# RWKV7 with a gated feed-forward on one core: weights converted by VectorE and ScalarE, in four parts, with the second stage starting two chunks earlier

## The chip, the cores and the metric

The kernel runs on one core of a Trainium2 chip. The metric is the device time of one execution in microseconds (us). Before the change three runs took 1106.02, 1109.82 and 1111.58 us, median 1109.82. A core has five engines with an instruction stream each: TensorE (PE, with its weight loads, PEld, shown apart), VectorE (DVE), ScalarE (ACT), GpSimd (POOL) and SyncE (SP), which here only issues DMAs. They meet through semaphores.

## The reference

Two stages. The first is a recurrence over 768 tokens for 4 batches and 8 heads of width 40; its output, as 3072 tokens of 320 numbers, is the input of a feed-forward with g = h·cos(h):

```python
for t in range(S):
    y[:, :, t] = np.einsum('bhd,bhde->bhe', rt, state)
    Sa = np.einsum('bhde,bhe->bhd', state, at)
    state_decay = state * wt[:, :, None, :] - np.einsum('bhd,bhe->bhde', Sa, bt)
    state = state_decay + np.einsum('bhd,bhe->bhde', vt, kt)
...
x = np.ascontiguousarray(attn_out.transpose(0, 2, 1, 3)).reshape(B * S, H * D)
...
h = x @ w_in
g = h * np.cos(h)
return (g @ w_out).astype(np.float32)
```

r, k, v, w, a, b are float32. w_in (320 x 2048) and w_out (2048 x 320) come as float64: the seeded array of float32 was multiplied by a float64 scalar. They are turned into float32 on the chip.

## The kernel before

**The recurrence** is cut into 24 chunks of 32 tokens (C = 32, NCH = 24). Chunk c works in segments. p1 prepares two chunks at a time: `p1_w` turns the decay w and scans it, `p1_a` makes the reciprocal `rw` and `aT`, `p1_b` turns `bn` into `bT`, `p1_n` makes the matrix `nps` from which `u` is filled through DRAM (`nd`). For four chunks at once a triangular system is inverted on VectorE in 31 steps of two instructions (`inv_step`, lines 309 and 313; tiles `inv_tmp` and `inv`), and sent through DRAM (`rd`) into `rt` (lines 317 and 320). p2 prepares one chunk: `p2_v` loads k, v and r of the next chunk and has GpSimd copy v and r into the padded tiles `vp` and `rp` (line 331), which TensorE turns to `vT` and `rT`; `p2_k` and `p2_g` follow. The chain that carries the state from chunk to chunk is `ch_t` (TensorE turns the state, `sT`, line 385: the mark by which a chunk's beginning is read), `ch_q` (`qps`), `ch_x` (`x0ps`, and x copied by ScalarE and VectorE), `ch_s` (`sps` with `rt`, then `sm`), `ch_z` (`dps`, the new state `qz` and the output `yt`). The output goes through DRAM (`xd`, line 492) into `xT` (lines 499 and 501), which holds two chunks.

**The second stage** (called MoE in the names) works on 12 groups of two chunks, g, and four blocks of 512 hidden columns, j. For each of the 48 pairs `first_a` and `first_b` make `ph` = w_in times xT (24 matmuls: 16 with `w_in_sb`, 8 with `w_in_tail`), ScalarE and VectorE turn it into g·cos (tiles `turns` and `gT`), and `second`, twice, adds `gT` times `w_out_sb` to `po` (16 matmuls). These four calls are pieces, 192 in all. They are laid between the segments of the chunks by a rule: from chunk START on, after each segment, as many as are due by SHARE pieces per chunk, and none of a group before the chunk that follows its second one. The rest comes behind chunk 23.

**The order.** TensorE keeps the order of the program text, segment by segment. The other engines' instructions are ordered by a scheduler, each engine then runs its own in that order.

**The weights.** `load_weights` (before the loop over chunks) goes through four blocks j; each has seven conversions by `rounded`: two of `w_in_sb` (128 x 512), one of `w_in_tail` (128 x 256), four of `w_out_sb` (128 x 320). A conversion loads the 64-bit words by a DMA of ScalarE's queue (line 163) into a tile `words` that shares the two buffers of `gT`; mantissa (`mant`, in the three buffers of `turns`) and exponent (`expo`, in the two buffers of `nt`) are taken apart by VectorE (lines 168, 169, 173, 178), scaled by ScalarE (line 172), the exponent is limited and moved by GpSimd (lines 176, 177), and GpSimd multiplies both (line 181). `kept` makes tiles that live throughout, and fills them by VectorE.

Of the kernel before, what the change touches and what calls it, by code (L numbers as in the profile page):

```python
# [20 lines left out]
def kernel(  # L21
# [63 lines left out]

    def kept(name, shape, n=1, fill=None, part=lambda t: t):

        tiles = []
        for i in range(n):
            t = const.tile(shape, F32, tag=f"{name}{i}", name=f"{name}{i}")  # L90
            if fill is not None:
                nc.vector.memset(part(t), fill)
            tiles.append(t)
        return tiles
# [21 lines left out]
    def load(c, names, via=nc.sync):  # L116
        for n in names:
            for i in range(B):
                via.dma_start(
                    nat[n][c % 2][blk[i], :, :D],  # L120
                    src[n][i, :, c * C : (c + 1) * C, :].rearrange("h t d -> t h d"),
                )
# [19 lines left out]
    rnd = kept("rnd", [P, 1], 1, ROUND)[0]  # L142
    w0 = kept("w0", [P, 4 * B, C], 1, 0.0)[0]
    w1 = kept("w1", [P, 4 * B, C], 1, 0.0)[0]
    bn_b = kept("bn", [P, H, DP], 7, 0.0, padding)
# [8 lines left out]
    by_in = kept("by_in", [P, 1], 1, 0.5 / math.pi)[0]  # L154
    by_out = kept("by_out", [P, 1], 1, 2.0 * math.pi)[0]

    def rounded(dst, src, by, by_sb):


        n, wid = dst.shape[0], dst.shape[-1]  # L160
        words = sb2.tile([P, 512, 2], I32, tag="gT", name="words")[:n, :wid]
        for rows, part in src:
            nc.scalar.dma_start(words[rows].rearrange("p n w -> p (n w)"), part.bitcast(I32))
# [4 lines left out]
        nc.vector.tensor_scalar(mant, hi, 0xFFFFF, None, ALU.bitwise_and)  # L168
        nc.vector.scalar_tensor_tensor(
            frac, lo.bitcast(U32), 2.0**-32, mant, ALU.mult, ALU.add  # L170
        )
        nc.scalar.activation(frac, frac, ACTF.Identity, bias=by_sb[:n], scale=2.0**-20 * by)
        nc.vector.tensor_scalar(
            expo, hi, 20, 0x7FF, ALU.logical_shift_right, ALU.bitwise_and
        )
        nc.gpsimd.tensor_scalar(expo, expo, 1023.0 + 128, 1023.0 - 127, ALU.min, ALU.max)
        nc.gpsimd.tensor_scalar(expo, expo, 127.0 - 1023, 2.0**23, ALU.add, ALU.mult)
        nc.vector.scalar_tensor_tensor(
            expo, hi, -(2**31), expo, ALU.bitwise_and, ALU.bitwise_or
        )  # L180
        nc.gpsimd.tensor_tensor(dst, frac, expo.bitcast(F32), ALU.mult)

    def load_weights():

# [9 lines left out]

        for j in range(NF // 4):
            cs = slice(4 * j * P, 4 * (j + 1) * P)
            for i in range(2):
                put(w_in_sb[:, i, cs], [(every, moe_w_in[i * P : (i + 1) * P, cs])], 0.5 / math.pi, by_in)
            put(
                w_in_tail[:, j].rearrange("p f n -> p (f n)"),  # L200
                [
                    (full[e], moe_w_in[2 * P :, (4 * j + 2 * e) * P : (4 * j + 2 * e + 2) * P])
                    for e in range(2)
                ],
                0.5 / math.pi, by_in,
            )
            for f in range(4 * j, 4 * j + 4):
                put(w_out_sb[:, f, :], [(every, moe_w_out[f * P : (f + 1) * P, :])], 2.0 * math.pi, by_out)

# [117 lines left out]
    def p2_v(c):  # L327
        load(c + 1, "kvr") if c + 1 < NCH else None
        nc.gpsimd.tensor_tensor(unpad(kn_b[c % 2]), unpad(nat["k"][c % 2]), G["rw", c], ALU.mult)  # L329
        for dst, m in ((vp, "v"), (rp, "r")):  # L330
            nc.gpsimd.tensor_copy(  # L331
                dst.rearrange("p (i f) d -> p f i d", f=2)[:, :, :, :D],
                nat[m][c % 2].rearrange("p (f i) d -> p f i d", f=2),
            )
        nc.gpsimd.tensor_copy(vvm[c % 2][:, :, C : C + D], nat["v"][c % 2])
        ps = at("vT")
# [245 lines left out]
    with tc.manual_schedule(engines={mybir.EngineType.PE}):  # L582
# [78 lines left out]
```

## Time and profile before

| what | before |
|---|---|
| runs | 1106.02, 1109.82, 1111.58 us; median 1109.82 |
| the profiled execution | 1102.25 us |
| its span on the core | 1100.5 us |
| mean granted TensorE clock | 0.812 |
| busy TensorE, VectorE, ScalarE, GpSimd | 74%, 46%, 31%, 21% |
| chunk 1 opens (first sT) | 178.33 us |
| chunk 2, chunk 3, chunk 4 open | 213.67, 231.93, 260.05 us |
| chunk 23 opens | 1020.8 us |

A row of the timeline reads: start in us, length in us, engine, line, operation, output<-inputs, shape, count, and in brackets the idle time of the engine before it with what ended it. A row of a group reads: line, engine, operation, shape and count, then total busy us and the mean ns of one, then the idle time just before them with its causes. A row of the stretches reads: from:to, length, then busy time (and number of instructions) of PE, PEld, DVE, ACT and POOL, the granted TensorE clock as a share of full speed, the DMA engines' busy share and GB/s.

### The profile page before, as it was taken

Reading aid. Unit: us, or ns where it says so; the run is one execution under the profiler, and the core shown is the slowest. Engines: PE = TensorE matmul, PEld = TensorE weight load, DVE = VectorE, ACT = ScalarE, POOL = GpSimd, SP = SyncE. Lnnn points to the kernel's source line nnn. Section 1 sums busy time; section 2 is a strip of 40 time slices with the busy share of each in tenths; the row PEclk is TensorE's granted clock in tenths of the full one; section 3 lists DMA queues with packets and bytes.
Section 4 is the critical chain, followed back from the end, with each engine's and each line's share of the span. In section 5 each row is a group of like instructions: output and inputs, shape, how many; then the busy total and the mean of one; then the engine's idle time right before and its main releaser. Section 6 shows DMA issues by size and latency. Waiting matters only on the chain.

```text
span 1100.5 us, 36921 instructions
## 1 busy us (share of the span) xinstructions
PE 819.2 (74%) x16472; PEld 630.7 (57%) x16472; DVE 511.2 (46%) x1107; ACT 342.4 (31%) x651; POOL 233.9 (21%) x414
## 2 busy tenths in 40 slices
PE   4310036666897898887888797797897789998997
PEld 3210035555676666665666666675665567776775
DVE  6489662464525563424572424662424662333221
ACT  2021121123233424232433242333232333434443
POOL 2454651312203012112011202111202111111000
PEclk8555556556888988797988988997889989998999
DMA  4554533235123323232232223141221221000000
GB/s 98 84 126 107 141 79 61 45 65 98 23 45 62 52 65 70 41 64 60 42 65 53 35 48 76 30 88 34 40 52 34 38 68 36 28 16 8 22 26 13
DMA packets 235519, 61.66 MB, mean 56 GB/s; under 512 B 209504, under 2 KB 229472, under 8 KB 235360
## 3 DMA queue, kind: packets, MB, share of 16 engines
q1 hardware_dynamic: 229088, 48.48, 23.4%
q10 hardware_dynamic: 6272, 10.82, 3.3%
q8 instruction: 130, 2.13, 0.8%
q14 instruction: 29, 0.24, 0.1%
HBM read 45.09 MB, written 14.16 MB: 54 GB/s over the span
## 4 chain that ended last, share of the span: by engine, by line
PE 59%; DVE 19%; ACT 8%; DMA 5%; issue 5%; POOL 3%; SPq 1%; ACTq 0%; DVEq 0%; POOLq 0%
PE ph L97 20%; PE po L97 19%; DVE inv L313 4%; DVE inv_tmp L309 3%; PE gram L97 3%; DVE rw L251 3%; PE x0ps L97 3%; PE vT L216 2%; ACT turns L529 2%; ACT turns L530 2%; PE sT L385 2%; PE dps L97 2%; PE nps L97 2%; PE bT L216 2%; PE qps L97 2%
## 5 line engine op out<-in xcount | busy, mean ns | idle before, releaser
L97 PE MATMUL po<-w_out_sb,gT 128*128 128x320 f32 x768 | 250.0, 479 | 2.3 <-issue 2.3
L97 PE MATMUL ph<-xT,w_in_sb 128*128 128x256 f32 x768 | 198.5, 410 | 0.5 <-issue 0.5
L97 PEld LDWEIGHTS po<-w_out_sb,gT 128*128 128x128 f32 x768 | 155.5, 211 | 71.6 <-issue 27.2
L528 DVE SCALAR_TENSOR_TENSOR turns<-turns,ph 128x512 f32<-128x512 f32 x96 | 61.6, 683 | 233.4 <-ACT turns L527 233.4
L97 PEld LDWEIGHTS ph<-xT,w_in_sb 128*128 128x128 f32 x768 | 154.7, 207 | 26.6 <-issue 0.9
L527 ACT ACTIVATE turns<-ph,rnd 128x512 f32<-128x512 f32 x96 | 60.7, 684 | 160.6 <-PE ph L97 160.6
L531 DVE TENSOR_TENSOR gT<-ph,turns 128x512 f32<-128x512 f32 x96 | 65.8, 689 | 63.0 <-ACT turns L530 62.7
L313 DVE TENSOR_TENSOR inv<-inv,inv_tmp 128x31 f32<-128x31 f32 (+15 forms) x186 | 73.8, 397 | 5.0
L309 DVE TENSOR_TENSOR inv_tmp<-u,inv 128x31 f32<-128x31 f32 (+15 forms) x186 | 70.7, 380 | 5.1
L530 ACT ACTIVATE turns<-turns,half_pi 128x512 f32<-128x512 f32 x96 | 68.9, 722 | 2.1
L97 PE MATMUL gram<-aT,kT 40*32 40x32 f32 x1536 | 20.1, 224 | 58.4 <-DVE yt L481 41.5
L529 ACT ACTIVATE turns<-turns 128x512 f32<-128x512 f32 x96 | 59.5, 623 | 13.1 <-DVE turns L528 13.1
L475 POOL TENSOR_TENSOR qz<-qz,wc 128x160 f32<-128x160 f32 x92 | 40.0, 460 | 105.2 <-DVE qz L474 105.1
L239 POOL COPY wx<-wp 128x496 f32<-128x496 f32 x24 | 14.8, 615 | 212.7 <-DVE wp L235 211.4
L251 DVE RECIPROCAL rw<-wn 128x320 f32<-128x320 f32 x24 | 51.6, 2150 | 12.1 <-PE wn L216 12.0
L97 PE MATMUL ph<-xT,w_in_tail 64*128 64x256 f32 x384 | 56.3, 413 | 0.0
L97 PEld LDWEIGHTS gram<-aT,kT 40*32 40x32 f32 x1536 | 17.3, 125 | 63.1 <-issue 42.3
L216 PE MATMUL vT<-ident,vp 128*128 128x128 f32 x96 | 18.0, 319 | 46.3 <-POOL vp L331 46.3
L329 POOL TENSOR_TENSOR kn<-nat_k,rw 128x320 f32<-128x320 f32 x24 | 21.0, 873 | 142.1 <-PE dps L97 142.0
L331 POOL COPY vp<-nat_v 128x320 f32<-128x320 f32 x24 | 10.9, 455 | 184.9 <-PE vT L216 72.2
L216 PE MATMUL vT<-ident,rp 128*128 128x128 f32 x96 | 17.2, 310 | 43.9 <-POOL rp L331 43.9
L264 ACT COPY bT<-bT 128x512 f32<-128x512 f32 x24 | 14.0, 585 | 110.8 <-PE bT L216 110.8
(94 smaller groups left out, 1170.9 us busy)
## 6 DMA issues: line engine op xcount, KB each, us to landing
words<-in_moe_w_out_dram ACTq DMA_DIRECT2D x16, 320.0 KB
words<-in_moe_w_in_dram ACTq DMA_DIRECT2D x8, 512.0 KB
nat_w<-in_w_dram SPq DMA_DIRECT2D x96, 40.0 KB
nat_b<-in_b_dram SPq DMA_DIRECT2D x96, 40.0 KB
nat_k<-in_k_dram SPq DMA_DIRECT2D x96, 40.0 KB
nat_v<-in_v_dram SPq DMA_DIRECT2D x96, 40.0 KB
nat_r<-in_r_dram SPq DMA_DIRECT2D x96, 40.0 KB
xd<-yt SPq DMA_DIRECT2D x48, 80.0 KB
```

The costliest lines, as they stand in the source:

```text
L97: nc.tensor.matmul(o, lhsT=lhsT, rhs=rhs, start=start, stop=stop, skip_group_check=True)
L216: nc.tensor.transpose(ps[:, i * P : (i + 1) * P], x[:, 2 * i : 2 * i + 2].rearrange("p e d -> p (e d)"), ident)
L251: nc.vector.reciprocal(rw, unpad(ps[:, 0].rearrange("p (h d) -> p h d", h=H)))
L309: nc.vector.tensor_tensor(tmp, u[:, :j, j : j + 1].to_broadcast([P, j, C - j]), x[:, j : j + 1, j:].to_broadcast([P, j, C - j]), ALU.mult,)
L313: nc.vector.tensor_tensor(x[:, :j, j:], x[:, :j, j:], tmp, ALU.subtract)
L385: nc.tensor.transpose(ps[:, i // 4, (i % 4) * P : (i % 4 + 1) * P], qz[:, i // 2, i % 2, C : C + P], ident)
L475: nc.gpsimd.tensor_tensor(z, z, wc.rearrange("p (f m b) -> p f m b", f=2, m=2)[:, :, :, bb] .unsqueeze(3).to_broadcast([P, 2, 2, D]), ALU. ...
L527: nc.scalar.activation(n, u, ACTF.Identity, bias=rnd, scale=1.0)
L528: nc.vector.scalar_tensor_tensor(n, n, -ROUND, u, ALU.add, ALU.subtract)
L529: nc.scalar.activation(n, n, ACTF.Abs)
L530: nc.scalar.activation(n, n, ACTF.Sin, bias=half_pi, scale=-2.0 * math.pi)
L531: nc.vector.tensor_tensor(G["gT", j][:, 2 * e : 2 * e + 2].rearrange("p f t -> p (f t)"), u, n, ALU.mult)
```

## The change

Five edits. **Conversion:** GpSimd's three steps go. The exponent is taken first; limiting and moving it is one Relu of ScalarE with the bias tile `to_bits`, and the last multiply is VectorE's. `expo` has buffers of its own. **Parts:** `load_weights` takes a block j; block 0 is converted before the loop, block c at the beginning of chunk c for c = 1, 2, 3. **START** is 2 instead of 4, so SHARE is 7.71 pieces per chunk instead of 8.48. **Fills** are GpSimd's but for three tiles. **k, v, r** have one buffer instead of two, and the next chunk's loads stand behind the copies in `p2_v`.

```diff
-    def kept(name, shape, n=1, fill=None, part=lambda t: t):
+    def kept(name, shape, n=1, fill=None, part=lambda t: t, on=nc.gpsimd):
...
-                nc.vector.memset(part(t), fill)
+                on.memset(part(t), fill)
...
-    nat = {n: kept(f"nat_{n}", [P, H, DP], 2, 1.0 if n == "w" else 0.0, padding) for n in "wabk"}
-    nat |= {n: kept(f"nat_{n}", [P, H, D], 2) for n in "vr"}
+    nat = {n: kept(f"nat_{n}", [P, H, DP], 2, 1.0, padding, nc.vector) for n in "w"}
+    nat |= {n: kept(f"nat_{n}", [P, H, DP], 2, 0.0, padding) for n in "ab"}
+    nat |= {n: kept(f"nat_{n}", [P, H, D], 1) for n in "kvr"}
...
+    to_bits = kept("to_bits", [P, 1], 1, (127.0 - 1023) * 2**23)[0]
...
-        expo = sb2.tile([P, 512], I32, tag="nt", name="expo")[:n, :wid]
+        expo = sb2.tile([P, 512], I32, tag="expo", name="expo")[:n, :wid]
         frac = mant.bitcast(F32)
+        nc.vector.tensor_scalar(
+            expo, hi, 20, 0x7FF, ALU.logical_shift_right, ALU.bitwise_and
+        )
+        nc.scalar.activation(expo, expo, ACTF.Relu, bias=to_bits[:n], scale=2.0**23)
         nc.vector.tensor_scalar(mant, hi, 0xFFFFF, None, ALU.bitwise_and)
         nc.vector.scalar_tensor_tensor(
             frac, lo.bitcast(U32), 2.0**-32, mant, ALU.mult, ALU.add
         )
         nc.scalar.activation(frac, frac, ACTF.Identity, bias=by_sb[:n], scale=2.0**-20 * by)
-        nc.vector.tensor_scalar(
-            expo, hi, 20, 0x7FF, ALU.logical_shift_right, ALU.bitwise_and
-        )
-        nc.gpsimd.tensor_scalar(expo, expo, 1023.0 + 128, 1023.0 - 127, ALU.min, ALU.max)
-        nc.gpsimd.tensor_scalar(expo, expo, 127.0 - 1023, 2.0**23, ALU.add, ALU.mult)
         nc.vector.scalar_tensor_tensor(
             expo, hi, -(2**31), expo, ALU.bitwise_and, ALU.bitwise_or
         )
-        nc.gpsimd.tensor_tensor(dst, frac, expo.bitcast(F32), ALU.mult)
-
-    def load_weights():
+        nc.vector.tensor_tensor(dst, frac, expo.bitcast(F32), ALU.mult)
+
+    def load_weights(j):
...
     def p2_v(c):
-        load(c + 1, "kvr") if c + 1 < NCH else None
...
+        nc.gpsimd.tensor_copy(vvm[c % 2][:, :, C : C + D], nat["v"][0])
+        if c + 1 < NCH:
+            load(c + 1, "kvr")
...
-        load_weights()
-
-        START, done = 4, 0
+        load_weights(0)
+
+        START, done = 2, 0
...
+            if 0 < c < NJ:
+                load_weights(c)
```

What this does to the order of an engine is seen in three places. On VectorE, at the beginning of the first inverse (lines 309 and 313; the other rows are conversions), the order before is:

```order
L168 TENSOR_SCALAR mant<-words 128x512
L173 TENSOR_SCALAR expo<-words 128x512
L309 TENSOR_TENSOR inv_tmp<-u,inv 128x31
L169 SCALAR_TENSOR_TENSOR mant<-words,mant 128x512
L313 TENSOR_TENSOR inv<-inv,inv_tmp 128x31
L309 TENSOR_TENSOR inv_tmp<-u,inv 128x60
L313 TENSOR_TENSOR inv<-inv,inv_tmp 128x30x2
L178 SCALAR_TENSOR_TENSOR expo<-words,expo 128x512
L309 TENSOR_TENSOR inv_tmp<-u,inv 128x87
L168 TENSOR_SCALAR mant<-words 128x512
```

and at the same place of the changed program, where lines 170, 174, 175, 179 and 182 are a conversion's five VectorE steps:

```order
L170 TENSOR_SCALAR expo<-words 128x320
L174 TENSOR_SCALAR mant<-words 128x320
L175 SCALAR_TENSOR_TENSOR mant<-words,mant 128x320
L179 SCALAR_TENSOR_TENSOR expo<-words,expo 128x320
L182 TENSOR_TENSOR w_out_sb<-mant,expo 128x320
L309 TENSOR_TENSOR inv_tmp<-u,inv 128x31
L313 TENSOR_TENSOR inv<-inv,inv_tmp 128x31
L309 TENSOR_TENSOR inv_tmp<-u,inv 128x60
L313 TENSOR_TENSOR inv<-inv,inv_tmp 128x30x2
```

Before, conversions and steps of the inverse alternate. After, 21 conversions (blocks 0, 1 and 2, though two of these blocks stand in the loop in the program's text) come ahead of the first step, and no conversion stands among the steps; the fourth block's seven stand behind the second inverse, in chunk 3.

On TensorE, chunk 2 before runs, from its sT on:

```order
L385 MATMUL sT<-ident_133,qz_107 128x128 x8
L97 MATMUL qps<-rT,s 64x32 x32
L216 MATMUL vT<-ident_133,vp_101 128x128 x4
L216 MATMUL vT<-ident_133,rp_103 128x128 x4
L97 MATMUL x0ps<-vvm_106,ag 32x72 x32
L97 MATMUL x0ps<-qz_107,aT 32x72 x32
L97 MATMUL sps<-x_2537,rt 32x72 x32
```

and after:

```order
L386 MATMUL sT<-ident_128,qz_102 128x128 x8
L97 MATMUL ph<-xT,w_in_sb 128x256 x8
L97 MATMUL ph<-xT,w_in_tail 128x256 x4
L97 MATMUL qps<-rT,s 64x32 x32
L216 MATMUL vT<-ident_128,vp_96 128x128 x4
L216 MATMUL vT<-ident_128,rp_98 128x128 x4
L97 MATMUL ph<-xT,w_in_sb 128x256 x8
L97 MATMUL ph<-xT,w_in_tail 128x256 x4
L97 MATMUL x0ps<-vvm_100,ag 32x72 x32
L97 MATMUL x0ps<-qz_102,aT 32x72 x32
L97 MATMUL po<-w_out_sb,gT 128x320 x4
L97 MATMUL sps<-x_2075,rt 32x72 x32
```

Pieces of the first group now stand between the segments of chunk 2, the first of them directly behind sT. (The order counts instructions; the profile counts a matmul of 32-bit numbers twice.)

On VectorE of the changed program, chunk 3 has the fourth block's conversions directly behind the last step of the second inverse:

```order
L309 TENSOR_TENSOR inv_tmp<-u,inv 128x31
L313 TENSOR_TENSOR inv<-inv,inv_tmp 128x31
L170 TENSOR_SCALAR expo<-words 128x512
L174 TENSOR_SCALAR mant<-words 128x512
L175 SCALAR_TENSOR_TENSOR mant<-words,mant 128x512
L179 SCALAR_TENSOR_TENSOR expo<-words,expo 128x512
L182 TENSOR_TENSOR w_in_sb<-mant,expo 128x512
```

The `sm` of chunk 3 stands behind the fifth of these conversions, its `qz` and `yt` behind the seventh; their DMAs are issued by ScalarE behind the activations of a piece.

More of the change, by code (lines that the diff above doesn't have):

```diff
@@ L119, in load @@
                 via.dma_start(
-                    nat[n][c % 2][blk[i], :, :D],
+                    nat[n][c % len(nat[n])][blk[i], :, :D],
                     src[n][i, :, c * C : (c + 1) * C, :].rearrange("h t d -> t h d"),
@@ L142 @@
     rnd = kept("rnd", [P, 1], 1, ROUND)[0]
-    w0 = kept("w0", [P, 4 * B, C], 1, 0.0)[0]
-    w1 = kept("w1", [P, 4 * B, C], 1, 0.0)[0]
+    w0 = kept("w0", [P, 4 * B, C], 1, 0.0, on=nc.vector)[0]
+    w1 = kept("w1", [P, 4 * B, C], 1, 0.0, on=nc.vector)[0]
     bn_b = kept("bn", [P, H, DP], 7, 0.0, padding)
@@ L193, in put @@
             nc.scalar.mul(dst, dst, by)
[L195 to L208, printed above, removed]
+        cs = slice(4 * j * P, 4 * (j + 1) * P)
+        for i in range(2):
+            put(w_in_sb[:, i, cs], [(every, moe_w_in[i * P : (i + 1) * P, cs])], 0.5 / math.pi, by_in)
+        put(
+            w_in_tail[:, j].rearrange("p f n -> p (f n)"),
+            [
+                (full[e], moe_w_in[2 * P :, (4 * j + 2 * e) * P : (4 * j + 2 * e + 2) * P])
+                for e in range(2)
+            ],
+            0.5 / math.pi, by_in,
+        )
+        for f in range(4 * j, 4 * j + 4):
+            put(w_out_sb[:, f, :], [(every, moe_w_out[f * P : (f + 1) * P, :])], 2.0 * math.pi, by_out)
     def at(name):
```

5 lines of the change are left out of this document (2 added, 3 removed).

## The prediction

> **What bounds the kernel now.** I read the head of the page, then its forty slices, and then busy time by stretches and the timeline, because the mean hides two different kernels.
>
> ```profile
> span 1100.5 us, 36921 instructions
> PE 819.2 (74%) x16472; PEld 630.7 (57%) x16472; DVE 511.2 (46%) x1107; ACT 342.4 (31%) x651; POOL 233.9 (21%) x414
> PE   4310036666897898887888797797897789998997
> PEclk8555556556888988797988988997889989998999
> ```
>
> From slice 10 on (each is 27.5 us) TensorE is eight tenths busy; before that it is nearly empty, and its clock stands at one half from slice 1 to about slice 9. The stretches cut this at the transposes that open a chunk (L385): chunk 2 begins at 213.67, chunk 3 at 231.93, chunk 4 at 260.05.
>
> ```profile
> 90.00:120.00 30.00, 0.00 (x0) 0.00 (x0) 26.75 (x61) 3.78 (x7) 16.10 (x23) 0.50 0.45 121
> 120.00:150.00 30.00, 3.98 (x73) 3.19 (x76) 19.61 (x35) 6.49 (x12) 20.95 (x31) 0.50 0.53 136
> 213.67:231.93 18.26, 15.23 (x539) 12.65 (x533) 3.61 (x13) 4.20 (x9) 2.14 (x5) 0.50 0.37 71
> 231.93:260.05 28.12, 15.49 (x538) 12.52 (x533) 25.13 (x75) 4.58 (x10) 5.18 (x11) 0.50 0.40 68
> 260.05:312.30 52.25, 43.29 (x793) 34.02 (x789) 19.10 (x33) 17.95 (x34) 12.45 (x24) 0.80 0.33 67
> 522.50:561.10 38.60, 32.04 (x629) 24.82 (x627) 25.18 (x64) 11.64 (x22) 5.57 (x10) 0.90 0.26 42
> ```
>
> Columns: length, busy PE, weight loads, DVE, ACT, POOL, then clock, DMA share, GB/s. From 90 to 120 TensorE does nothing while VectorE is 89% busy. Chunks 2 and 3 hold attention alone; from chunk 4 MoE pieces are mixed in and TensorE has 7 to 9 us free per chunk. So before 150 us VectorE bounds, afterwards TensorE and the chain of a chunk.
>
> The timeline shows what ends the empty stretch (start, length, engine, operation, and in brackets the wait before it):
>
> ```profile
> 10.76 0.43 DVE L168 TENSOR_SCALAR mant<-words 128x512 int32<-128x512 int32 x1 [3.23 <-DMA words<-in_moe_w_in_dram]
> ...
> 68.23 0.20 DVE L309 TENSOR_TENSOR inv_tmp<-u,inv 128x31 f32<-128x31 f32 x1
> ...
> 115.03 0.19 DVE L313 TENSOR_TENSOR inv<-inv,inv_tmp 128x31 f32<-128x31 f32 x1
> 115.25 0.34 SPq L317 DMA_DIRECT2D rd<-inv  x1
> ...
> 123.31 10.77 SPq L119 DMA_DIRECT2D nat_r<-in_r_dram  x3
> 145.03 0.54 POOL L331 COPY rp<-nat_r 128x320 f32<-128x320 f32 x1
> 145.62 1.11 PE L216 MATMUL vT<-ident,rp 128*128 128x128 f32 x4 [22.19 <-POOL rp L331]
> 149.10 1.25 PE L97 MATMUL sps<-x,rt 32*32 32x72 f32 x64 [1.51 <-ACT rT L342]
> 232.70 0.19 DVE L309 TENSOR_TENSOR inv_tmp<-u,inv 128x31 f32<-128x31 f32 x1
> ...
> 257.37 0.19 DVE L313 TENSOR_TENSOR inv<-inv,inv_tmp 128x31 f32<-128x31 f32 x1
> ```
>
> The first inverse takes 47.0 us (68.23 to 115.22), shared with conversions; the second takes 24.9 us with VectorE mostly to itself. Only then do `rd` and the loads of `nat_r` behind it on SP go out, and chunk 0's `sps` runs at 149.1.
>
> **Part by part: the conversions.** One conversion of a w_out block, before:
>
> ```profile
> 126.39 0.33 ACTq L163 DMA_DIRECT2D words<-in_moe_w_in_dram  x1
> 126.66 0.91 DVE L168 TENSOR_SCALAR mant<-words 128x320 int32<-128x320 int32 x1 [0.30 <-DMA words<-in_moe_w_out_dram]
> 127.49 0.31 DVE L173 TENSOR_SCALAR expo<-words 128x320 int32<-128x320 int32 x1
> 127.72 0.48 DVE L169 SCALAR_TENSOR_TENSOR mant<-words,mant 128x320 f32<-128x320 uint32 x1
> 128.30 0.56 ACT L172 ACTIVATE mant<-mant,by_out 128x320 f32<-128x320 f32 x1 [2.65 <-DVE mant L169]
> 129.09 0.49 DVE L178 SCALAR_TENSOR_TENSOR expo<-words,expo 128x320 int32<-128x320 int32 x1 [0.88 <-POOL expo L177]
> 129.73 0.88 POOL L181 TENSOR_TENSOR w_out_sb<-mant,expo 128x320 f32<-128x320 f32 x1 [0.68 <-DVE expo L178]
> 130.33 0.56 DVE L168 TENSOR_SCALAR mant<-words 128x512 int32<-128x512 int32 x1 [0.75 <-DMA words<-in_moe_w_in_dram]
> ```
>
> The three GpSimd steps go. Two operations have no row before. The multiply on VectorE lies between 0.31 (L173) and 0.88 us (L181 on GpSimd); I take 0.48, the two-input L169. Relu on ScalarE lies between 0.31 (L173) and 0.88; I take 0.56, L172's. VectorE's own work is then 0.31 + 0.31 + 0.48 + 0.49 + 0.48 = 2.1 us, and with the last ScalarE step and its hand-overs about 2.5 (a 320-wide block), 3.05 (512) and 2.7 (a tail): 2 × 3.05 + 2.7 + 4 × 2.5 = 18.8 us a part. At the bounds of the multiply a put is 0.2 shorter or 0.4 longer: −4 to +8 us over 21 puts.
>
> **The order of the conversions.** In the order of the changed program three of the four parts (21 puts) stand ahead of the first inverse on VectorE, so its stretch isn't spared them, only the fourth; but behind them the inverse runs alone. VectorE's other work there is p1(0) and p1(2), with four of these:
>
> ```profile
> L251 DVE RECIPROCAL rw<-wn 128x320 f32<-128x320 f32 x24 | 51.6, 2150 | 12.1 <-PE wn L216 12.0
> L92 DVE MEMSET bn<- 128x192 f32 x7 | 1.5, 218 | 0.0
> ```
>
> 4 × 2.15 = 8.6, and about as much for scans, aT and nt (estimate): 17 us. The first words land at 10.8: 10.8 + 3 × 18.8 + 17 ≈ 84. Then 24.9 gives 109, against 115.2: 6 us. More goes behind it: copies of `rp` and `vp` no longer stand between conversions on GpSimd, and chunk 1's r, queued behind rd and rt, has the DMA engines without words beside it. From rd to `rp` took 29.8 us; with the row's 10.8 us wait for three issues mostly gone I expect 15, so `rp` at 124 and `sps` at 127: **−22 us**, between 0 (29.8 stays, and the multiply at its upper bound eats the 6) and −30 (`rp` 10 us behind rd, the multiply at its lower bound). Chunks 0 and 1 keep their TensorE order and lose 1 us, since no conversion runs beside them; chunk 2 opens at 191 instead of 213.7.
>
> **Fills.** Some sixteen memsets like that of `bn` at 0.22 us, 4 to 5 us with the larger ones (estimate), leave VectorE ahead of 10.8, where it waits 3.2 us for words anyway; on GpSimd they stand before the product into `bn`, which costs 0 to 5 us in p1(0), beside conversions. I take 0. The single k, v, r buffers move SP's loads behind p2_v's copies; a load then has a whole chunk, 18 us in the shortest. I take 0, at worst a stall of 2 us in each of chunks 1 to 3 (6 us).
>
> **MoE two chunks earlier.** SHARE falls from 8.48 to 7.71 pieces per chunk, and 14 of 192 (four `ph` sets, three `po` sets) now stand before chunk 4. Their size, per set of 24 ph or 16 po matmuls:
>
> ```profile
> L97 PE MATMUL po<-w_out_sb,gT 128*128 128x320 f32 x768 | 250.0, 479 | 2.3 <-issue 2.3
> L97 PE MATMUL ph<-xT,w_in_sb 128*128 128x256 f32 x768 | 198.5, 410 | 0.5 <-issue 0.5
> L97 PE MATMUL ph<-xT,w_in_tail 64*128 64x256 f32 x384 | 56.3, 413 | 0.0
> ```
>
> A ph set is (198.5 + 56.3) / 48 = 5.3 us, a po set 250.0 / 48 = 5.2: 4 × 5.3 + 3 × 5.2 = 36.8 us leave chunks 4 to 23. Their idle time stays, because it stands where the chain has no pieces beside it, so I pass 0.9 of it on: −33. But xT is asked for earlier:
>
> ```profile
> 213.67 1.97 PE L385 MATMUL sT<-ident,qz 128*128 128x128 f32 x8
> ...
> 215.95 1.11 SPq L501 DMA_DIRECT2D xT<-xd  x2
> ```
>
> With the first ph directly behind chunk 2's sT, the loads of xT leave 2.3 us after it opens, and TensorE waits 3.5 us (estimate). The next groups' first pieces stand likewise directly behind sT of chunks 4 and 6 or near it in later ones, about 3 us each for two: +6. Of the 2.65 us that one set of chunk 4 lost to a half clock (6.27 against 3.62 in the rows below) 2 are paid earlier now: −2. Chunks 4 to 23: **−29 us**.
>
> ```profile
> 264.24 3.62 PE L97 MATMUL ph<-xT,w_in_sb 128*128 128x256 f32 x16
> 267.80 1.14 PE L97 MATMUL ph<-xT,w_in_tail 64*128 64x256 f32 x8
> ...
> 274.64 0.84 PE L97 MATMUL gram<-aT,kT 40*32 40x32 f32 x60 [4.06 <-ACT kT L348]
> ...
> 276.12 6.27 PE L97 MATMUL ph<-xT,w_in_sb 128*128 128x256 f32 x16
> ...
> 285.94 4.47 PE L97 MATMUL po<-w_out_sb,gT 128*128 128x320 f32 x16
> ```
>
> At full clock a ph set takes 4.7 us (264.24 to 268.94), a po set 4.5. Chunk 2 gets three and one, 18.6 us: 18.3 + 18.6 + 3.5, less 1 for attention work at a raised clock, is 39.4: **+21**, so chunk 3 opens at 231, as now.
>
> **Chunk 3** gets part 3's seven puts. They are queued behind the inverse for chunk 4 on VectorE, their DMAs on ScalarE behind the pieces' activations, and six of seven use one buffer of `gT` one after another. A round is the load (126.39 to 130.33 is 3.9 us for 512 columns; 3.2 for 320, from the put before) plus the four steps that read words: 6.1 us for a 512, 4.6 for the tail, 5.1 for a 320: 2 × 6.1 + 4.6 + 4 × 5.1 = 37 us in series. They start when po j1 leaves the buffer, 5.5 us in; w_in stands complete at about 19 and 24, `sm` is behind the fifth put, `qz` and `yt` behind the seventh (43), and gram and the next sT follow. About 49 us against 28.1: **+21**, so chunk 4 opens at 279 against 260: +19.
>
> Sum: −22 + 21 − 1 + 21 = +19 at chunk 4, −29 after it: **−10 us** on the profiled execution's 1102.25 (span 1100.5, 1.75 outside), 1092. The median, 1109.8, lies 7.6 above that execution, so on its footing **1099**.
>
> **Rivals.** *The series of part 3 decides (slower).* It is a single chain of DMA, VectorE and ScalarE through one buffer in the middle of chunk 3, with TensorE waiting for w_in and for the state behind it. If the 37 us stand wholly beside no TensorE work, chunk 3 takes 28 + 37 = 65, chunk 4 opens at 295, 35 late, and −29 leaves +6 to +8; with the bound of the multiply, +15. It decides from chunk 4 opening after 289, the 29 late. For it: the order puts qz and yt behind all seven. Against: pieces of j1 and j2 are ready to fill. 1116 to 1125.
>
> *The inverse isn't earlier (same).* At the upper bound 21 puts last 8 us longer and the inverse ends at 117; the first term shrinks to about −14 and the pass-through of 36.8 to 0.8: −10 + 8 = −2, 1108. The four parts then don't do what they say: three are still ahead of the first inverse.
>
> *The conversions hide (faster).* Chunk 3 resembles the later chunk with an inverse, 38.60 us with 32.04 of TensorE (last row of the stretches): +10 rather than +21, and p2's loads save a few more: −10 − 11 − 4 = −25, 1085.
>
> *The clock doesn't rise (slower).* In chunk 2 TensorE was busy 15.2 of 18.3 us and the clock stayed at 0.50. In chunk 4 the same 16 matmuls took 3.62 and, behind a wait of 4.06 us, 6.27 us. Before chunk 4, 4 × 4.7 + 3 × 4.5 = 32 us of pieces at 6.27 / 3.62 = 1.73 cost 23 us more: −10 + 23 = +13, 1122. Against: the first pieces of chunk 4 took 3.62 at once. The Trainium skill ("TensorE: Matmul & The Clock Gate", Part 1: The HAM clock gate) says that the clock is halved after an idle window of about 3.4 us and full after one such window of sustained activity; by it pieces broken by waits for xT and w_in would run partly at half clock, and this rival would be likelier. The trace agrees at the 6.27 us behind the wait of 4.06, and not in chunk 2, where TensorE was busy 83% of 18.3 us in small matmuls and had no full clock.
>
> **How the numbers follow.** Forecast 0.35 (1092 to 1108, 0.27 of it below 1104.3), hiding 0.23, inverse not earlier 0.17, series 0.17, clock 0.08. A measurement tells about 0.5%, 5.5 us, from no change, that is outside 1104.3 to 1115.3. Faster: 0.27 + 0.23 + 0.03 = 0.53. Same: 0.08 + 0.12 + 0.03 = 0.23. Slower: 0.02 + 0.14 + 0.08 = 0.24. The range runs from 1075 (hiding with the multiply at its lower bound and the best prologue) to 1121 (series), leaving about 0.1 at each end.
>
> **What would show it.** Right: the first inverse lasts under 27 us and ends by 110; `sps` of chunk 0 at about 127; chunk 2 of 36 to 43 us; chunk 3 of 44 to 54 us with TensorE waiting for w_in_sb; later chunks 1.2 to 1.7 us shorter. Wrong: inverse after 115, chunk 3 near 38 or 65 us, clock 0.50 through chunk 2's pieces, or later chunks unchanged.

## The result and the profile after

The changed kernel takes 1077.34 us (median; 1071.70 to 1084.64), the kernel before 1109.21 in the same comparison. The ratio is 0.9718, 95% interval 0.9651 to 0.9785: 2.8% faster, inside the range and on the side that was forecast, but about three times the forecast 10 us and only 2 us inside the fast end of the range. The profiled execution of the changed kernel took 1084.64 us, the slowest of its four, that of the kernel before 1102.25, faster than its median; read from the two traces the gain is 17.6 us, and the other 14 lie in which executions were profiled.

The head of the page after, and its slices:

```profile
span 1082.9 us, 36890 instructions
PE 820.3 (76%) x16472; PEld 628.6 (58%) x16472; DVE 505.2 (47%) x1112; ACT 355.8 (33%) x679; POOL 179.0 (17%) x352
PE   4221366856679698788879879878987979999998
PEclk9999995877798798887898889889899989899999
```

GpSimd has lost 55 us of work and VectorE none to speak of; TensorE's busy time is the same. What moved is where the empty slices end: TensorE reaches six tenths in slice 5 instead of 6 and eight in slice 7 instead of 10, where pieces now stand.

The busy time by stretches (length, PE, PEld, DVE, ACT, POOL, clock, DMA share, GB/s), for two stretches of the beginning, chunk 2, chunk 3 and chunk 4:

```profile
60.00:90.00 30.00, 7.32 (x272) 5.93 (x272) 24.41 (x62) 11.34 (x20) 3.63 (x5) 1.00 0.58 134
90.00:120.00 30.00, 2.21 (x68) 1.71 (x68) 16.80 (x48) 0.77 (x2) 2.81 (x5) 1.00 0.37 65
181.82:231.53 49.71, 35.69 (x626) 27.30 (x620) 26.82 (x69) 13.23 (x23) 5.80 (x10) 0.74 0.28 45
231.53:279.21 47.68, 26.84 (x591) 19.63 (x589) 27.52 (x71) 19.10 (x35) 5.67 (x11) 0.75 0.43 101
279.21:332.27 53.06, 44.02 (x804) 34.09 (x797) 17.90 (x31) 15.59 (x31) 9.36 (x18) 0.87 0.29 58
```

Chunk 2 opens at 181.8 instead of 213.7, 32 us early; chunk 3 at 231.5 as before (231.9); chunk 4 at 279.2, 19 us late; and the 20 chunks and the rest behind it take 803.7 us instead of 840.4. So the gain is made twice and given back once, in chunks 2 and 3.

The timeline of the beginning:

```profile
84.26 0.20 DVE L309 TENSOR_TENSOR inv_tmp<-u,inv 128x31 f32<-128x31 f32 x1
...
108.02 0.19 DVE L313 TENSOR_TENSOR inv<-inv,inv_tmp 128x31 f32<-128x31 f32 x1
108.24 0.34 SPq L317 DMA_DIRECT2D rd<-inv  x1
...
116.83 1.87 SPq L120 DMA_DIRECT2D nat_r<-in_r_dram  x4
...
119.04 1.12 PE L216 MATMUL vT<-ident,vp 128*128 128x128 f32 x4 [21.74 <-POOL vp L330]
...
120.75 0.46 POOL L330 COPY rp<-nat_r 128x320 f32<-128x320 f32 x1 [1.36 <-DMA nat_r<-in_r_dram]
...
123.54 1.26 PE L97 MATMUL sps<-x,rt 32*32 32x72 f32 x64 [0.31 <-ACT rT L343]
```

The first inverse has VectorE to itself, 23.9 us instead of 47.0, and the four issues of `nat_r` behind it take 1.87 us where three took 10.77 before.

Chunk 2, TensorE's rows with a wait or a low pace:

```profile
181.82 1.97 PE L386 MATMUL sT<-ident,qz 128*128 128x128 f32 x8
186.97 5.28 PE L97 MATMUL ph<-xT,w_in_sb 128*128 128x256 f32 x16 [3.18 <-DMA xT<-xd]
...
198.79 6.18 PE L97 MATMUL ph<-xT,w_in_sb 128*128 128x256 f32 x16 [3.39 <-DVE gT L532]
...
224.67 0.82 PE L97 MATMUL gram<-aT,kT 40*32 40x32 f32 x60 [6.39 <-DVE yt L482]
...
226.14 3.78 PE L97 MATMUL ph<-xT,w_in_sb 128*128 128x256 f32 x8
```

Sixteen ph matmuls take 5.28 and 6.18 us, and half as many 3.78, where the full pace is 3.62 for sixteen. Three waits make 13 us: for xT, for `gT` (a set's activations must end before the next set has a PSUM buffer) and for `yt`, which VectorE works out among the steps of the second inverse. The granted clock (third number from the right) was 0.50, 1.00 and 0.50 in these stretches:

```profile
181.82:190.18 8.36, 5.18 (x22) 4.18 (x17) 0.76 (x2) 1.07 (x2) 0.00 (x0) 0.50 0.49 102
190.18:197.01 6.83, 5.22 (x90) 4.05 (x88) 1.28 (x2) 3.48 (x5) 0.46 (x1) 1.00 0.74 73
197.01:203.84 6.83, 5.05 (x12) 4.09 (x13) 1.38 (x2) 2.98 (x6) 0.45 (x1) 0.50 0.37 60
```

So the first set began at half pace, as sT ahead of its wait had (1.97 us for eight transposes, 1.09 where chunk 3 opens), and the clock fell again 1.6 us into the second wait, which began at 195.40.

Chunk 3:

```profile
236.97 0.38 ACTq L165 DMA_DIRECT2D words<-in_moe_w_in_dram  x1
241.38 0.43 DVE L170 TENSOR_SCALAR expo<-words 128x512 int32<-128x512 int32 x1 [1.73 <-DMA words<-in_moe_w_in_dram]
243.50 0.33 ACTq L165 DMA_DIRECT2D words<-in_moe_w_in_dram  x1
247.47 0.43 DVE L170 TENSOR_SCALAR expo<-words 128x512 int32<-128x512 int32 x1 [3.13 <-DMA words<-in_moe_w_in_dram]
250.56 2.07 PE L97 MATMUL ph<-xT,w_in_sb 128*128 128x256 f32 x4 [4.08 <-DVE w_in_sb L182]
268.19 0.98 PE L97 MATMUL dps<-vvm,kn 32*64 32x72 f32 x53 [0.83 <-DVE sm L448]
277.74 0.82 PE L97 MATMUL gram<-aT,kT 40*32 40x32 f32 x60 [7.48 <-DVE yt L482]
```

The first six loads of the fourth block go out 4.7 to 6.5 us apart, each only when the conversion before it has left the one buffer; TensorE waits for `w_in_sb` twice (5.38 and 4.08 us), and at the end 7.48 us for `yt` behind the seventh conversion.

### The profile page after: what moved, and what is told of

Same layout as the page of the kernel before. It is cut to its first block, busy times and chain, and to the rows that moved or that the text cites. A ratio compares the mean times of both kernels' runs of the same rounds, so it can differ in the third digit from the quotient of the medians.

```text
span 1082.9 us, 36890 instructions
## 1 busy us (share of the span) xinstructions
PE 820.3 (76%) x16472; PEld 628.6 (58%) x16472; DVE 505.2 (47%) x1112; ACT 355.8 (33%) x679; POOL 179.0 (17%) x352
## 4 chain that ended last, share of the span: by engine, by line
PE 54%; DVE 20%; ACT 11%; DMA 8%; issue 4%; POOL 2%; SPq 1%; ACTq 0%; DVEq 0%; POOLq 0%
PE ph L97 20%; PE po L97 16%; DVE inv_tmp L309 3%; DVE inv L313 3%; PE gram L97 3%; DMA words<-in_moe_w_in_dram 3%; DVE rw L251 3%; ACT turns L531 3%; DMA words<-in_moe_w_out_dram 3%; PE x0ps L97 3%; ACT turns L530 3%; DVE wp L235 2%; PE vT L216 2%; PE qps L97 2%; PE sT L386 2%
## 5 line engine op out<-in xcount | busy, mean ns | idle before, releaser
L97 PE MATMUL ph<-xT,w_in_sb 128*128 128x256 f32 x768 | 208.9, 426 | 20.3 <-DVE w_in_sb L182 9.5
L97 PEld LDWEIGHTS ph<-xT,w_in_sb 128*128 128x128 f32 x768 | 160.3, 215 | 50.7 <-DVE w_in_sb L182 10.4
L313 DVE TENSOR_TENSOR inv<-inv,inv_tmp 128x31 f32<-128x31 f32 (+15 forms) x186 | 68.4, 368 | 5.7
L378 ACT COPY vvm<-gram 128x256 f32<-128x256 f32 x24 | 8.9, 372 | 137.9 <-DVE vvm L374 137.9
L216 PE MATMUL bT<-ident,bn 128*128 128x128 f32 x96 | 22.4, 377 | 33.3 <-POOL bn L256 11.2
L239 POOL COPY wx<-wp 128x496 f32<-128x496 f32 x24 | 15.0, 626 | 193.2 <-DVE wp L235 190.8
L97 PEld LDWEIGHTS ph<-xT,w_in_tail 64*128 64x128 f32 x384 | 34.6, 195 | 20.0 <-issue 17.2
```

Source lines behind the costliest of these rows:

```text
L97: nc.tensor.matmul(o, lhsT=lhsT, rhs=rhs, start=start, stop=stop, skip_group_check=True)
L216: nc.tensor.transpose(ps[:, i * P : (i + 1) * P], x[:, 2 * i : 2 * i + 2].rearrange("p e d -> p (e d)"), ident)
L313: nc.vector.tensor_tensor(x[:, :j, j:], x[:, :j, j:], tmp, ALU.subtract)
```

## The experiments

Times are medians, each beside runs of the kernel before of its own comparison (1107 to 1110); "sps" is when chunk 0's `sps` runs, "opens" the sT of chunk 2 or 4, "rest" from there to the end of the profiled span.

| run | us | ratio to before (interval) | sps | 2 opens | chunk 2 | chunk 3 | 4 opens | rest |
|---|---|---|---|---|---|---|---|---|
| before | 1109.2 | | 149.1 | 213.7 | 18.3 | 28.1 | 260.1 | 840.4 |
| the change | 1077.3 | 0.9718 (0.9651 to 0.9785) | 123.5 | 181.8 | 49.7 | 47.7 | 279.2 | 803.7 |
| e1 START 4 | 1082.7 | 0.9774 (0.9728 to 0.9820) | 133.2 | 193.2 | 17.7 | 27.6 | 238.4 | 840.3 |
| e2 before, START 2 | 1088.6 | 0.9837 (0.9769 to 0.9906) | 149.1 | 211.7 | 48.5 | 25.0 | 285.1 | 802.4 |
| e3 GpSimd converts | 1093.2 | 0.9868 (0.9811 to 0.9925) | 135.2 | 194.4 | 49.7 | 52.6 | 296.6 | 795.0 |
| e4 block 3 early | 1071.9 | 0.9672 (0.9624 to 0.9721) | 135.0 | 195.6 | 48.7 | 24.2 | 268.4 | 805.0 |
| e5 fills on VectorE | 1078.7 | 0.9775 (0.9697 to 0.9853) | 124.7 | 183.4 | 49.7 | 46.6 | 279.7 | 797.9 |
| e6 expo in nt | 1082.7 | 0.9802 (0.9733 to 0.9871) | 105.0 | 176.6 | 57.7 | 45.1 | 279.4 | 797.7 |
| e8 that, blocks early | 1071.5 | 0.9692 (0.9612 to 0.9771) | 113.2 | 196.5 | 49.1 | 24.4 | 270.0 | 802.2 |
| e9 spread | 1076.0 | 0.9727 (0.9661 to 0.9793) | 115.8 | 196.4 | 50.2 | 24.4 | 271.0 | 802.8 |
| e11 no low words | 1075.3 | 0.9686 (0.9631 to 0.9741) | 120.3 | 179.5 | 49.3 | 45.0 | 273.7 | 801.4 |
| e14 one block | 1031.1 | 0.9302 (0.9231 to 0.9374) | 96.9 | 156.5 | 49.0 | 25.0 | 230.5 | 795.2 |
| e12 START 3 on e4 | 1058.8 | 0.9543 (0.9478 to 0.9609) | 136.0 | 195.8 | 17.5 | 45.5 | 258.8 | 790.9 |
| e13 START 2.2 on e4 | 1046.6 | 0.9429 (0.9372 to 0.9487) | 134.2 | 194.3 | 42.3 | 31.1 | 267.8 | 776.6 |

The rest of the change and of e5, e6 is the same TensorE order; it took 803.7, 797.9 and 797.7, so about 6 us of a rest are the execution's, not the kernel's.

**e1, START at 4 again.**

```diff
-        START, done = 2, 0
+        START, done = 4, 0
```

> The changed kernel with START at 4 again; everything else stays. Theory A (the gain is the shorter prologue; pieces in chunks 2 and 3 cost there about what they save later): chunk 2 back to about 18 us, chunk 3 to 28 to 34, chunks 4 to 23 back to about 840 us, prologue late by up to 12 us because the fourth block's seven conversions now stand among the steps of the first inverse; total 1080 to 1092 us, against 1077 for the change. Rival B (the gain comes from the pieces standing earlier): 1100 us or more.

1082.7 us, as theory A had it. The rest is back at 840.3 against 840.4 of before, so the 37 us that the change saves there belong to START. Conversion, parts and fills without START are worth 26 us.

**e2, START at 2 in the kernel before.**

```diff
-        START, done = 4, 0
+        START, done = 2, 0
```

> The kernel before with START at 2 and nothing else. Theory A: chunk 0's sps stays at about 149 us, chunks 2 and 3 grow by 35 to 45 us together, less than the 51 of the change since all weights are converted by then, and chunks 4 to 23 shrink by about 37; total within 10 us of before, 1100 to 1115. Rival B (earlier pieces are the gain): 1085 or less.

Theory A missed, and 1088.6 lies between it and rival B, nearer to B: a gain of 20 us (13 by the traces). Chunk 2 pays 30.2, chunk 3 gains 3.1, so the two grow by 27.1 and not by 35 to 45; the rest gains 38.0, and chunk 2 opens 2 us earlier. Early pieces are a gain by themselves. One reason is in the second inverse, beside which TensorE has little to do: chunk 3 of before has it busy 15.5 of 28.1 us, and in its timeline stands a wait for x, which VectorE copies among the steps of that inverse:

```profile
251.10 1.24 PE L97 MATMUL sps<-x,rt 32*32 32x72 f32 x62 [7.57 <-DVE x L426]
```

In this run the inverse lies beside the pieces of chunk 2, and chunk 3 lasts 25.0 with pieces in it. The gains of e1 and e2 add up to 46, the change has 32. By the traces the sum is 34.4 against 17.6, so 16.8 are lost together: chunk 3 loses 23.2 more than the two alone, the beginning gains 9.4 more, the other stretches make up 3.

**e3, GpSimd converts again, in four parts.**

```diff
+        nc.gpsimd.tensor_scalar(expo, expo, 1023.0 + 128, 1023.0 - 127, ALU.min, ALU.max)
+        nc.gpsimd.tensor_scalar(expo, expo, 127.0 - 1023, 2.0**23, ALU.add, ALU.mult)
...
-        nc.vector.tensor_tensor(dst, frac, expo.bitcast(F32), ALU.mult)
+        nc.gpsimd.tensor_tensor(dst, frac, expo.bitcast(F32), ALU.mult)
```

> The changed kernel with the conversion of before (three steps on GpSimd, the last multiply too), in four parts and with START 2. Theory A: a conversion lasts 3.1 to 3.6 us instead of 2.3 to 2.7, so the first inverse begins 12 to 20 us later (96 to 104 us instead of 84) and the total is 1087 to 1097. Rival C (it is the order alone, inverse behind the conversions and not among them, that shortens the prologue): the same as the change, 1077 within 5. Rival D: no gain left, 1105 or more.

1093.2 us, as theory A had it; the inverse begins at 95.4, just ahead of its 96 to 104. Its timeline:

```profile
95.44 0.20 DVE L310 TENSOR_TENSOR inv_tmp<-u,inv 128x31 f32<-128x31 f32 x1
...
119.87 0.19 DVE L314 TENSOR_TENSOR inv<-inv,inv_tmp 128x31 f32<-128x31 f32 x1
...
128.68 1.87 SPq L120 DMA_DIRECT2D nat_r<-in_r_dram  x4
...
135.16 1.26 PE L97 MATMUL sps<-x,rt 32*32 32x72 f32 x64 [0.31 <-ACT rT L344]
```

The inverse begins 11.2 us later than in the change and ends even 4.8 us later than before; still `sps` comes 13.9 us earlier than before. So of the 25.6 us by which the change brings `sps` forward, 11.6 belong to the conversion without GpSimd and 13.9 to what e3 keeps: above all the order, by which no words are loaded and nothing is converted behind the inverse. From the end of the first inverse to `sps` it is 33.9 us before, with ten conversions in that stretch, and 15.3 in the change and 15.1 in e3, with none. Before, two things stand there. SP's issues of `nat_r` take 0.3 us each, but between them SP waits for loads of words to land (SP's waits from 115 to 135 us: sum, times, longest):

```profile
SPq L119 <- DMA words<-in_moe_w_in_dram: 9.8, 2, 6.6
```

The last of these issues ends at 134.1 us, and GpSimd copies `rp` only at 145.0, behind the steps of three more conversions. The single buffers of k, v and r weren't tried apart, but they don't shorten the stretch by themselves: e9 has them too, and five conversions behind the inverse, and takes 24.9 us.

**e4, the fourth block with the third.**

```diff
-            if 0 < c < NJ:
-                load_weights(c)
+            if c == 1:
+                load_weights(1)
+            if c == 2:
+                load_weights(2)
+                load_weights(3)
```

> The changed kernel with the fourth block converted together with the third one, ahead of the first piece in the program, so that its words take their buffer before gT does. By the order its seven conversions then stand among the steps of the first inverse. Theory A (the series of seven conversions through one buffer costs chunk 3 about 14 us): chunk 3 at 30 to 36 us instead of 47.7, the first inverse's end 14 to 20 us later than 108, total 1075 to 1085. Rival E (the series is covered by TensorE work and costs nothing): chunk 3 stays above 44 us and the total is 1090 or more.

Rival E falls: the series does cost time. Theory A has the direction, and with 13.9 us nearly the 14 to 20 by which the inverse ends later, but the other two numbers were missed on the fast side: chunk 3 lasts 24.2 us and not 30 to 36, and the total is 1071.9 and not 1075 to 1085. The stretches of chunk 2 and chunk 3:

```profile
195.62:244.27 48.65, 35.77 (x627) 27.51 (x621) 25.60 (x65) 13.22 (x23) 5.80 (x10) 0.77 0.26 43
244.27:268.44 24.17, 22.74 (x591) 17.39 (x589) 13.68 (x39) 11.54 (x21) 3.94 (x8) 1.00 0.38 77
```

Chunk 3 falls from 47.7 to 24.2 us, TensorE busy for 22.7 of them, with the same 14 pieces ahead of chunk 4: the series of seven conversions cost it 23 us, not the 14 of the expectation. The same seven, one ahead of the first inverse and six among its steps, cost 13.8 there (chunk 2 opens at 195.6). That is where e1 and e2 lose together, since with START 2 the pieces take the buffers first and push the fourth block into chunk 3. In the total, 5 us less than the change; the intervals overlap.

**e5, fills on VectorE.**

```diff
-    def kept(name, shape, n=1, fill=None, part=lambda t: t, on=nc.gpsimd):
+    def kept(name, shape, n=1, fill=None, part=lambda t: t, on=nc.vector):
```

> The changed kernel with the fills on VectorE again (kept's default engine). Theory A (the fills are hidden, VectorE waits for the first words until 10.5 us anyway, while about 5 us of fills end before that): first conversion within 1 us of 10.5, first inverse at 84 to 86 us, total 1077 within 5. Rival F (fills held up the conversions): first inverse 4 us later or more, total 1082 or more.

Nothing: 1078.7, the inverse at 85.6 instead of 84.3. Fills were hidden.

**e6, e8, e9: the inverse earlier.** With `expo` in the buffers of `nt` again, blocks 1 and 2 stay behind the first inverse, which begins at 64.5 (e6); e8 moves the blocks, e9 makes single conversions wait.

```diff
-        expo = sb2.tile([P, 512], I32, tag="expo", name="expo")[:n, :wid]
+        expo = sb2.tile([P, 512], I32, tag="nt", name="expo")[:n, :wid]
...
+        if gate is not None:
+            nc.gpsimd.tensor_copy(words[:, 0:1, 0], gate.bitcast(I32)[:n])
```

(the first edit in e6 and e8, where e8 also calls block 1 in chunk 0, blocks 2 and 3 in chunk 1; the second in e9)

> The changed kernel with expo sharing the two buffers of nt, as before the change, and nothing else. By the order the conversions of blocks 1 and 2 then stand behind the first inverse, in chunks 0 to 2, since nt of chunk 4's preparation takes those buffers first; chunk 3 keeps its seven conversions. Theory A (the 14 conversions ahead of the first inverse hold up the whole prologue): inverse from about 55 to 80 us, chunk 0's sps at 95 to 100 instead of 123.5; chunks 0 to 2 give 5 to 20 us of it back, chunk 4 opens at 255 to 270 instead of 279, total 1053 to 1068. Rival G (VectorE's work has to be done before chunk 2's pieces anyway): chunk 2 opens at 180 or later and the total is 1075 or more.

> As the run with expo in nt's buffers, and block 1 converted in chunk 0, blocks 2 and 3 in chunk 1 of the program, ahead of the first piece. By the order 14 conversions stand before the first inverse's end, 14 in chunks 0 and 1, none in chunk 3. Theory A: inverse from about 55 to 95 us, chunk 0's sps at 110, chunk 2 opens at 180 to 190, chunk 3 lasts 24 to 30 us instead of 47.7; total 1055 to 1066. Rival G: what chunk 3 loses chunks 0 and 1 gain, total 1075 or more.

> The changed kernel with the 28 conversions placed one by one: ten free, five behind the first inverse, three behind sm and three behind yt of chunk 0, two, three and two behind x0, sm and yt of chunk 1 (a copy of one element on GpSimd makes their words wait). Theory A: inverse from about 60 to 85 us, chunk 0's sps at about 100, chunk 2 opens at 165 to 175, chunk 3 lasts 24 to 30 us, total 1040 to 1055. Rival G (conversions delay chunks 0 and 1 by as much as the prologue gains): chunk 2 opens at 182 or later, total 1062 or more, all of the gain over the change from chunk 3.

Theory A missed in all three; rival G's totals came in e6 and e9, and e8's 1071.5 lies between the two. `sps` comes 8 to 19 us earlier than in the change, and by chunk 4 this is gone: e6 opens it at 279.4 as the change does, e8 and e9 at 270.0 and 271.0 as e4 does (268.4). A conversion that is taken out of the way of the first inverse stands in the way of chunks 0 to 2 instead: from `sps` to the opening of chunk 2 it is 58.3 us in the change, and 71.7, 83.4 and 80.7 in e6, e8 and e9, which have 7, 14 and 11 conversions in that stretch. e9's timeline shows one form of it:

```profile
90.90 0.34 SPq L325 DMA_DIRECT2D rd<-inv  x1
...
96.23 5.45 SPq L328 DMA_DIRECT2D rt<-rd  x4
...
102.97 5.34 SPq L120 DMA_DIRECT2D nat_v<-in_v_dram  x4
...
110.97 1.11 PE L224 MATMUL vT<-ident,vp 128*128 128x128 f32 x4 [31.03 <-POOL vp L338]
```

With five conversions and their loads behind the inverse, `sps` follows its end by 25 us (115.8) instead of the change's 15: the four issues of `nat_v` take 5.34 us, where the change's took 1.87. SP's waits from 90 to 110 us say why; the change has none for words there:

```profile
SPq L328 <- DMA words<-in_moe_w_out_dram: 4.2, 2, 3.6
SPq L120 <- DMA words<-in_moe_w_in_dram: 3.6, 1, 3.6
SPq L120 <- DMA words<-in_moe_w_out_dram: 3.5, 1, 3.5
```

**e11, one VectorE step less; e14, one block alone.** e11 leaves out the low words, so weights keep 20 bits; e14 fills the weights of blocks 1 to 3 with a constant.

```diff
-        nc.vector.scalar_tensor_tensor(
-            frac, lo.bitcast(U32), 2.0**-32, mant, ALU.mult, ALU.add
-        )
...
+                if j:
+                    nc.gpsimd.memset(dst, 0.01)
+                else:
+                    rounded(dst, src, by, by_sb)
```

(the first edit is e11's, with mant going into the activation, the second e14's)

> The changed kernel without the step that adds the low word of each weight: of a conversion's five VectorE steps one (0.49 us at 320 columns, 0.69 at 512) is left out, so weights keep 20 bits of mantissa. Theory A (VectorE's own time per conversion sets when the first inverse begins): 21 steps of 0.5 us, first inverse at 72 to 76 us instead of 84, chunk 0's sps at 112 to 116, chunk 3 shorter by 2 to 3, total 1062 to 1068. Rival H (the loads of the words set the cadence): first inverse at 82 or later, total 1074 or more.

> The changed kernel with block 0 alone converted; the weights of blocks 1 to 3 are filled with a constant by GpSimd, so 21 of 28 conversions and their loads are left out. It prices what the conversions still cost. Theory A: first inverse at about 55 us, chunk 0's sps at 90 to 95, chunk 2 opens at 150 to 158 instead of 182 and still lasts 46 to 50, chunk 3 lasts 24 to 26 instead of 47.7; chunk 4 opens at 222 to 234 instead of 279, total 1020 to 1035. Rival I (the chain of the chunks bounds, conversions lie beside it): chunk 4 opens at 255 or later, total 1050 or more.

e11: the inverse begins at 81.2, 3 us earlier and not 10; the total lies within the change's interval. Neither theory has it whole. Ahead of the first inverse VectorE is busy 9.9 us less (54.4 instead of 64.3) and idle 6.8 us more (26.8 instead of 19.9). The step that was left out had covered ScalarE's step on `expo`; now VectorE waits for that (the group behind it, 320 columns, whole run, the change and then e11):

```profile
L179 DVE SCALAR_TENSOR_TENSOR expo<-words,expo 128x320 int32<-128x320 int32 x16 | 7.7, 482 | 0.0
```

```profile
L176 DVE SCALAR_TENSOR_TENSOR expo<-words,expo 128x320 int32<-128x320 int32 x16 | 8.2, 510 | 4.2 <-ACT expo L173 3.9
```

Over all widths, ahead of the inverse, this wait is 6.5 us instead of 0.2, the waits for words 17.5 instead of 14.0, and the waits for `mant`, 3.7 us in the change, are nearly gone. e14: 1031.1, as theory A had it: the inverse begins at 57.2, held by u's load alone:

```profile
57.16 0.20 DVE L312 TENSOR_TENSOR inv_tmp<-u,inv 128x31 f32<-128x31 f32 x1 [7.41 <-DMA u<-nd]
```

Chunk 4 opens 48.7 us earlier than in the change. That is what 21 conversions still cost, 2.3 us each, and e6 to e9 show that moving them saves little of it: 8 to 11 us in e4, e8 and e9, nothing in e6.

**e12 and e13, START at 3 and at 2.2 on e4.**

```diff
-        START, done = 2, 0
+        START, done = 2.2, 0
```

(3 in e12)

> The kernel with the fourth block converted ahead of the first piece (run e4), and START at 3: seven pieces instead of 14 before chunk 4. Theory A (early pieces gain because they stand beside the second inverse, about 25 us of VectorE in which TensorE is otherwise idle half the time; half of them in chunk 3 does the same): chunk 2 at 18 us, chunk 3 at 40 to 46, chunks 4 to 23 at 820 to 825, total within 5 of e4's 1072. Rival J (each early piece is worth the same, half of them half the gain): 1077 to 1083.

> The kernel of run e4 with START at 2.2, so that the first piece of a group no longer stands directly behind sT of chunk 2, where TensorE waited 3.2 us for xT. Theory A: that wait goes, chunk 2 at 43 to 47 us instead of 48.7, the later groups' the same in part, total 1062 to 1070. Rival K (the wait moves to the next piece, or to yt behind the inverse): 1070 to 1074.

Both are well below what was expected, and e13 is the fastest that was run: 1046.6 us, interval 0.9372 to 0.9487, clear of the change's, and 25 us less than e4. Yet the beginning gave nothing: chunk 4 opens at 267.8 in e13 and 268.4 in e4. The gain is in the rest. The stretch from chunk 4 to the end in e4 and then e13:

```profile
268.44:1073.40 804.96, 689.54 (x13560) 526.13 (x13556) 341.64 (x744) 278.52 (x533) 130.09 (x240) 0.89 0.25 47
```

```profile
267.79:1044.40 776.61, 670.26 (x13557) 512.65 (x13555) 339.97 (x742) 279.42 (x532) 128.95 (x237) 0.92 0.27 49
```

The same matmuls keep TensorE busy 19.3 us less at a clock of 0.92 instead of 0.89, and its idle time falls by 9 us (115.4 to 106.4). Part of this is the execution's: nine other runs with START 2 have TensorE busy 681.6 to 691.7 us in rests of 795.0 to 803.7, so e13 lies 11 and 18 us below the lowest. The waits of ph for xT (sum, times, longest), first e4, then e13:

```profile
PE ph L97 <- DMA xT<-xd: 8.0, 3, 4.2
```

```profile
PE ph L97 <- DMA xT<-xd: 0.8, 1, 0.8
```

START moves the phase and the pace together: at 2.2 SHARE is 7.78 instead of 7.71, so the first piece comes a fifth of a chunk later and the shift shrinks to nothing by chunk 23. By the traces it is worth 28 us, most of it in TensorE's pace. Chunks 4 to 7 hold the same 32 pieces in both runs and take 156.3 us in e13, 171.3 in e4: 15 of the 28 us. By the rule START 2 has no piece left for the last segment of chunks 3 and 5 and then puts three directly behind the next sT, where TensorE waits 4.2 and 1.7 us for xT; START 2.2 has pieces in those segments, and its one such wait is 0.8. That these places are the cause is argued; no run changes them alone.

e12 says that the number of early pieces isn't what counts. By the rule it has nine of them before chunk 4, not the seven of the expectation (three ph sets and one and a half po sets, about 23.7 us), and its rest is 49.5 us shorter than before's. START 2, with fourteen, has 36.8 less in the change.

## Why the prediction came out as it did

**The prologue (−22): right, step by step.** The inverse was to begin at 84 and end at 109, `rp` to be copied at 124, `sps` to run at 127; they came at 84.3, 108.2, 120.8 and 123.5. The terms of the 84 hold one by one: the first words at 10.5 us, VectorE's other work 17.0, and 56.8 for the 21 conversions with their waits, against 10.8, 17 and 56.4. The order with 21 conversions ahead of the inverse was the key. The division held as well: the inverse ends 7.0 us earlier, and what follows it is 18.6 us shorter; in e3 the inverse ends later than before, and what follows it is as short. e5 confirms the fills at nothing. The rival that the inverse isn't earlier fell with this.

**Chunks 0 and 1 (−1): mis-sized.** From `sps` to chunk 2's sT the change takes 58.3 us, before 64.6: −6.3. In every run without a conversion between the first inverse and chunk 2 it is 58.3 to 60.6. The conversions and loads that ran up to there before are the likely price, of which the text put 1 us; no run takes it alone.

**Chunk 2 (+21): mis-sized, it measured +31.4.** The sum put three ph sets and a po set at full pace (18.6 us) and one wait of 3.5. The xT wait came as put (3.18). Two more were left out, 3.39 for `gT` and 6.39 for `yt`, and the ph sets ran at a lower clock, which the text kept as a rival with 0.08 of the chance and not as a term. The waits weigh more: TensorE is idle 14.0 us in chunk 2, where the sum had 6.5, and busy 35.7, where it had 32.8. The Trainium skill, "TensorE: Matmul & The Clock Gate", Part 1: The HAM clock gate, has an idle window of about 3.4 us halve the clock. The measured rows agree in part: behind the wait of 3.39 us sixteen matmuls took 6.18 us instead of 3.62. But the clock fell 1.6 us into that wait, and the first set was slow because it began at half clock. The size was the same in every run with START 2, whatever the conversions did (48.5 to 50.2, but for e6, which converts in chunk 2), so it is the pieces' own.

**Chunk 3 (+21): right.** 47.7 us against 49, with the mechanism as told: one buffer, 6.1 to 6.5 us a round at 512 columns (6.1 in the text), `sm` behind the fifth, `yt` behind the seventh conversion. e4 takes it away and chunk 3 lasts 24.2. The rival by which this series decides needed chunk 4 to open after 289; it opened at 279.2, where the sum had put it. The rival that the conversions hide fell as well.

**Chunks 4 to 23 (−29): mis-sized, −36.8.** TensorE is busy 30.2 us less there and idle 6.6 less (691.7 of 803.7 us against 721.9 of 840.4). The text had the idle time unchanged and took 0.9 of the pieces' 36.8. The waits for xT came, 1.95 and 2.29 us in chunks 4 and 6, but other idle time fell by more. That the saving equals the length of the moved pieces is luck: e12 moves about 23.7 us of pieces and saves 49.5, e13 moves 36.8 and saves 63.8. The step that failed is that a moved piece saves its own length; where the pieces stand between the segments, and at what clock they run there, counts as much.

**The sum.** Terms of −25.6 − 6.3 + 31.4 + 19.6 − 36.8 give −17.7 on the profiled executions, for −10 forecast. Chunk 2 was 10.4 us too cheap, and the prologue, chunks 0 and 1, and chunk 3 were 3.6, 5.3 and 1.4 too dear: that chunk 4 opens at 279 as forecast is luck. The rest was 7.8 too dear. The step that failed worst is the footing: 7.6 us was added to go from one execution to the median, while the other kernel's profiled execution lay 7.3 above its own median. The measured 1077 lies nearer to the 1085 of the rival that the conversions hide than to 1099, but that rival's condition, a chunk 3 like the 38.6 us one, did not come.

## What to carry to other kernels

Before costing a move "beside other work", look at the order for who queues behind it on the engine and which ring of buffers it shares: a shared buffer (gT) pushed seven conversions into a chunk where they cost 23 us, and an unshared one (expo) let fourteen others run ahead of the first inverse. Work that an engine must finish before a common point cost about the same here wherever it was put ahead of that point (e6, e8, e9), so shorten it or move the point. Where fill-in work is laid between the links of a chain by a counter, try its phase before its amount: starting a fifth of a chunk later was worth 25 us here (e13 against e4), more than the 16 us of taking GpSimd out of the conversion (e3).

## What was not expected of the hardware

The granted clock shown for the nearly idle beginning says nothing of the pace there: it is 1.00 from 90 to 120 us in the change and 0.50 before, while four 128x128 transposes took 1.12 us in the change (119.0) and 1.11 before (145.6, also at 0.50), and 0.60 to 0.66 at full pace in chunk 2. The mean clock of a span, 0.884 against 0.812, overstates the difference for that reason; the stretches from chunk 4 on have 0.89 in both. Slow matmuls behind a wait need not be slow because of it: of two sets of sixteen in chunk 2 that took 5.28 and 6.18 us instead of 3.62, the first had begun at half clock before its wait. And SP's row for a few small loads stretches from 1.9 to over 5 and up to 10.8 us while the weights' words are being loaded, though each issue takes 0.3 to 0.8 us: between them SP waits for a load of words to land, which these loads don't need.
